# R by rows of eight tokens, W and R loaded singly, the last token's decay by one-column products, in a new order

## The chip, the cores and the metric

The kernel runs on one core of a Trainium2 chip. The time is that of one execution on the device in microseconds, the median of several runs. In a profile, PE is TensorE's matmuls, PEld its weight loads, DVE is VectorE, ACT is ScalarE, POOL is GpSimd, and SP is the engine whose queue issues most DMAs.

## What is computed

A recurrence over 768 tokens keeps a 40 x 40 state for each of 4 batches and 8 heads; its outputs go through a feed-forward block.

```python
for t in range(S):                       # S = 768, D = 40
    y[:, :, t] = np.einsum('bhd,bhde->bhe', rt, state)
    Sa = np.einsum('bhde,bhe->bhd', state, at)
    state_decay = state * wt[:, :, None, :] - np.einsum('bhd,bhe->bhde', Sa, bt)
    state = state_decay + np.einsum('bhd,bhe->bhde', vt, kt)
...
h = x @ w_in                             # x: 3072 x 320, w_in: 320 x 2048
g = np.maximum(h, 0.0) ** 2
return g @ w_out                         # 2048 x 320
```

## The kernel before

The 768 tokens are cut into 6 chunks of 128, and a chunk of one batch is a unit `m` (24 of them, in the code "batch" too). For each unit the six inputs W, K, B, A, V and R are loaded as tiles with 128 tokens on the partitions and 8 heads x 40 beside them (`NW`, `NK`, ... `NR`).

Preparation of a unit: ScalarE takes the logarithm of W (`ln`), a matmul with a triangle of ones (`cs`) sums it over the tokens into a PSUM bank, and two exponentials make the decays `GA` and `GI`. GpSimd or VectorE multiply K and B by `GI` (`kb`), and A by the decay that is shifted by one token (`aa`; from unit 6 a DMA makes the shifted `E` from `GA`). TensorE transposes A, K and B, V and R (`tA`, `tKB`, `tV`, `tR`), each by matmuls with the identity `IDb`; ScalarE or VectorE copy the results out of PSUM (`AT`, `KBT`, `VT`, `RT`). From unit 8 K and B are transposed by a DMA instead, on SP's queue. `GL` is the decay of a chunk's last token, one value for each of 320 columns with those on the partitions.

Two steps `st` per unit, of four heads each, then do the chunk's algebra: `ca` (products of 64 rows, two heads at once), the masks `CN`, the corrections `P`, `corr1`, `corr2` with `Mc`, `c1` and `Sn`, the products with R (`ex`), the masks `EVX`, the outputs and the next state (`y`, `Xn`, `us`, `UZ`). The feed-forward block of one or two units is `tx`, `XT`, `hr` (64 rows), `hp`, `hs` (relu), `Gt` (square), `op`, `osb` and the store.

TensorE has three arrangements here: the whole array (128\*128), rows cut in two (64\*128: `ca`, `ex`, `hr`), and rows and columns cut in two (64\*64: the transposes of R of units 0 to 3).

R of units 0 to 3 is loaded so that a partition holds 8 consecutive tokens of one head, a run of 320 floats; two DMAs of 64 partitions each do it (`rows`). `t_r` then makes 16 transposes of 64 by 64, and `e_r` reads the bank with a stride. R of later units is loaded with one token per partition, two units in one DMA (`two`), and `t_r` makes four transposes of 128 by 128. W's tiles are pairs of units too, two of them; a pair's tile is free for the next load when both units have used it. For units 0 to 5 `GL` comes from four matmuls of one column (`gl_mm`) that write into the bank of `cs`; from unit 6 a DMA transpose of `GA`'s last 32 tokens, one for two units, brings it into `GD`, and GpSimd or VectorE multiply that by the mask `HM`.

Each engine runs its instructions in the order that is written out in the table `ORDER`; `WAYS` says which of the possible engines makes an operation, `BANKS` which of the 8 PSUM banks it takes, and `IDLE` before which operations filler matmuls are put (`L1060`).

Of the kernel before, what the change touches and what calls it, by code (L numbers as in the profile page):

```python
# [7 lines left out]
FP32 = mybir.dt.float32  # L8
# [11 lines left out]
def kernel(  # L20
# [39 lines left out]
    RING = {"N": 3, "NW": 2, "lnW": 2, "GI": 2, "KB": 5, "GA": 2, "E": 3, "AA": 2, "V": 5, "R": 3, "SN": 8,  # L60
            "EVX": 3, "RT": 4, "VT": 4, "KBT": 3, "AT": 3, "GL": 4, "GD": 2, "CN": 3, "c1": 2, "x1": 2,
# [3 lines left out]
    SPLIT, THREE, ROWS, GLD, PAIR = 1, 6, 4, 6, 4  # L65
# [59 lines left out]
    def pe(n):  # L125
        return n, n + 0.165
# [130 lines left out]
    for m in range(NBC):  # L257
        o = Batch()
        bt.append(o)
        o.nat = bt[m - 1].nat if m % 2 else {key: buf(f"N{key}") for key in "WKBAVR"}  # L260
        o.lnW, o.hi, o.lo, o.GI, o.KB, o.AA, o.V, o.R, o.VT, o.RT, o.KBT, o.AT, o.GL, o.Xn = (
            buf(x) for x in ("lnW", "hi", "lo", "GI", "KB", "AA", "V", "R", "VT", "RT", "KBT", "AT", "GL", "Xn"))
        o.GA, o.E, o.GD = (bt[m - 1].GA, bt[m - 1].E, bt[m - 1].GD) if m % 2 else (buf(x) for x in ("GA", "E", "GD"))
# [20 lines left out]
    def add_load(m, key, rank):  # L284
        o = bt[m]
        c, bb = divmod(m, NB)

        def tile_():
            return sb(o.nat[key], [128, 2, NHH, D], FP32)

        def go():
            nc.sync.dma_start(
                out=tile_()[:, m % 2],
                in_=nat_srcs[key][bb, :, c * L:(c + 1) * L, :].rearrange("h t e -> t h e"))

        def two():
# [4 lines left out]
        def rows():  # L301
            t_ = tile_()[:, m % 2]
            src = nat_srcs[key][bb, :, c * L:(c + 1) * L, :]
            for s in range(2):
                nc.sync.dma_start(
                    out=t_[64 * s:64 * s + 64].rearrange("p i e -> p (i e)"),
                    in_=src.rearrange("(j s) (b i) e -> s b j (i e)", s=2, i=8)[s])
        if m >= PAIR and m % 2:
            alias["L", m, key] = "L", m - 1, key
            return  # L310
        op(("L", m, key), "SP", rank, 0.6, 0.6, [], [o.nat[key]],
           two if m >= PAIR else rows if key == "R" and m < ROWS else go)
        ops["L", m, key].dma = "h", 1.03

    def add_prep(m):
# [5 lines left out]
        def ln():  # L321
            t_ = sb(o.lnW, [128, NHH * D], FP32)
            nc.scalar.activation(out=t_[:], in_=o.nat["W"].tile[:, m % 2].rearrange("p h e -> p (h e)"),
# [55 lines left out]
        def gl_ev(eng, at):  # L379
            t_ = sb(o.GL, [128, PB, 2], FP32)  # L380
            engine(eng).tensor_tensor(
                out=t_[:], in1=HM[:], op=ALU.mult,
                in0=at.rearrange("p (j u) -> p j u", u=1).to_broadcast([128, PB, 2]))
        def gl_row():
            nc.sync.dma_start_transpose(out=sb(o.GD, [128, 2 * PB, 32], BF16)[:],
                                        in_=o.GA.tile[96:128].rearrange("p b h e -> p (b h e)"))
        if m < GLD:
            op(("gl", m), "PE", s0 - 0.5, *pe(0.102), [("GA", m), ("GI", m)], [o.GA, csb], gl_mm, "F")
            op(("GL", m), "DVE", s0 - 0.3, 0.075, 0.16, [("gl", m)] + cleared("HM", 0), [csb, o.GL],
               lambda: gl_ev("DVE", csb.tile[:, 320:320 + PB]))  # L390
        else:
            if m % 2:
                op(("gD", m), "SP", s0 - 2.0, 0.6, 0.6, [("GA", m - 1), ("GA", m)], [o.GA, o.GD], gl_row)
                ops["gD", m].dma = "h", 0.4
                alias["gD", m - 1] = "gD", m
            op(("GL", m), "POOL", s0 - 0.3, 0.1, 0.16, [("gD", m)] + cleared("HM", 0), [o.GD, o.GL],
               lambda eng: gl_ev(eng, o.GD.tile[:, PB * (m % 2):PB * (m % 2) + PB, 31]), alts=[("DVE", 0.075, 0.16)])
# [13 lines left out]
        def cast(key, j0, n, eng):  # L411
            h = slice(2 * j0, 2 * j0 + 2 * n)
            copy(eng, out=getattr(o, key).tile[:, h, 0:D], in_=o.nat[key].tile[:, m % 2, h])
# [102 lines left out]
        def e_r(eng):  # L516
            t_ = sb(o.RT, [128, PB, L], BF16)[:]
            if m >= ROWS:
                copy(eng, out=t_, in_=bank(b4)[:, 0:PB * L].rearrange("p (j t) -> p j t", t=L))
                return  # L520
# [3 lines left out]
           "R" if m < ROWS else "F")  # L524
# [404 lines left out]
    def add_guard():  # L929
# [32 lines left out]
        "#D!8!=!2!%!;!$!(#J!6#F!:!>!+!.#K$C!-!L!,!?!9!!!)!&#L#O!<!@!^!A#E!_!C#M!B#N#I!J!U#Q!M!7!D"  # L962
        "$I!I!E!H!5!S#G#P!O$J!T!Y!N$K%>!P!/!W!K!X#H!`#U!Z$N!a$D!r$P!3#T!b!c$O$F#X!t!V!F$Q!0!d$L#V"
        "&=!i!s!Q!e#[!f$M%A!*!R!g!u#Y!h!v#`#Z#]![!w%D!x#t!]%E#W$E#v%F#u#b$U$G!y#R!G#c%G!z#a#w#^#d"
        "!j%H%I#S!|!##e%K%B$S#f!k!}#x#_%?!~!{%P#g#y##$X$H#k$T#z!l#!($(%$R#h$Z&>!m(&#$$[$Y#{%@$V!n"
        "%J#&$a%Q$s#|&?%N#i$]#j$u&@#}%S!4#)$c#~&C%L!1%T#%(*%M$b#l$W%C$^$t$_$!$d!o&D#m!p$`$#&E!q$v"
        "&H$%$w%O$e$$#n&I$f%U#*(,$g#o$x&J$h$&$i&K#p%V&F#(((#/$y#q&M$)$j$z#r$(()#s$*%[${&G$k&L%^(+"
        "%n$l$})5%]$.$/(/#0$~&A%W$0#1%!$|%p(0(-$m%#%_&N%`%$%a(6$n%%(7(.%o&T$o&U#2%q%X$p(1%r#6$q&B"
        "%e$r#3%(%R&O(4%s#4&R(5%&#7#9%b%Y%)&S#5$+%c%t+*&n%Z);%u#=%v%d)<#:&p#+)v%f#;&o&Z):)=%*#>&]"
        "$1&P%+$2&[#8)>&q%g)w&^)7&r%h&_(2)x$3&V%j&`&s%w%x&a&Q$5&t)?(3%y&X)@&W#<(:%i&b%z&c&Y%{&#(<"  # L970
        "(;(8%|%k$6)6)y(=(9&u$4&e%}&v){%~$8%l&f#-$9&!(>&d&x)8#?(O%m&y$<(Q)z(?#,(P&g(@%,$:&h)|&((R"
        "$7&)$;(A%0$=&*(B%-(S&i+j#.(C(T+0%3(D&z)C&w*$&j&{%.%7*(%1(F(U#@&|(G+1%/+k(V&}(W(E%4&l&$&m"
        "%8(Y&k$?$>(X)~(Z)F(H%5([(J*/)B#A&~)}(!(I+2&+(^#B(#(K&&#C(]+l&/%2)I)9(g*#(_*0)J+.(h&%+3*%"
        "(`,y$@)D+5(j$-(M(c(a)G&,+4)H$A(L)O(i%6)c%9)Q(k&-*++,)e(l)M*&%:&0)d&.)E)P)N)f*))A&1*,)g++"
        ")R+m)S)h**+n)T)i(N*1)X)U*D(d*2)V)j+o%;*3)k+p)W-!*E(b)l)m&2*F%<)K*4-#+-)Y)L*5*G)n&6-]-$+q"
        "*H)Z*6)o&7+8*M&3)p+/+7)[&4*-*7*I)^*.(m+t+>(n)q(t+u*J*8(o)r*9&8(u)]+9*K(p.l*;(q)s*L(v*W,{"
        ")_*<*:)t*N)a*=*O-%&5+v+<+{-(&9+=(r)`+w*?$,*!)u+V*>+C-^)b(x+x+D-_*@(y+W&:+:+;+E(z(s,z-`*B"
        "-&+X*P*[&;({*X+r-b*A(|*R(w)!*Q/O+y-d+F-a+Y+z+?(}+A+Z*S,|+G+B+@+H+[*T*])#,~+I,#*_*^+J*`)$"
        "*U+K,7,%*a)%+L)&,$(~)*.r+]-c)(,&,8+M-++^/P+|+N+O+_,9,(-*)+*b*V,-,:*f+s))*C,;,),}+Q*c*g),"
        ",<+a-1*d,=*i+}*j+b-h,>,*+c*k,?.m,+-g+~,,*m+d(f$B,A-,+e,.,!*p+P-i*q*h-/-.+`*t*e*r-4.o-0+f"  # L980
        ",/-j+R.s-n+g-k-l.t+T-5+S--*l,B+h-6-m-I-8-2*n/Q-o-7)--p,N-J*u.q+6-9-K+U,0-:-e,C*o,1-q-;)."
        "-r,2,J-?-<.n,D-L-3-=,3,E%=->,O)//R-R,5,F,P,6,4-s(e,G.*+i)1.+,Q-M,K/S,H/T.,-N,R,@*w.p-O*s"
        ".u,S-u-P*{0d.w-t.--@..*x,I-Q-A./-S*y.0/U-B-T.})2-C*z-D.v-v*v.z.y-U,T-w*|,X-V/V-|-x.1.|,U"
# [185 lines left out]
```

## Time and profile before

| | |
|---|---|
| Median of 3 runs | 257.37 us (256.85 to 257.81) |
| Profiled execution, its own time | 256.97 us |
| Its span, first to last instruction | 255.4 us |
| Granted TensorE clock | 1.00 |
| DMA queue of SP, share of 16 engines' span | 76.5% |

A row of a group gives line, engine, operation, the tiles written and read, the number of instructions, then busy us and mean ns of one, and after the second bar the engine's idle time before them and what ended it. A row in order of time gives the start, the busy time of the merged group, engine, line and tiles. Matmuls are pipelined: the busy time of one holds its whole passage, so that what a matmul takes from TensorE is read from start to start.

### The profile page before, as it was taken

The numbers are of one execution on the slowest core, as the hardware profiler recorded it, in microseconds if no ns is written. First come the engines' busy times: TensorE is split into PE (matmuls) and PEld (weight loads), VectorE is DVE, ScalarE is ACT, GpSimd is POOL, SyncE is SP. The second block draws the span as 40 slices with busy tenths as digits, with TensorE's granted clock in tenths as the row PEclk, the third lists the DMA queues.
The fourth block names the chain that finished last, engine by engine and source line by source line (L and its number), as shares of the span: only waits on it lengthen the run. The fifth ranks groups of instructions, "written<-read, shape, count | busy, mean of one in ns | idle before, by whom it ended". The sixth has DMA issues, their size and how long they took to land.

```text
span 255.4 us, 9993 instructions
## 1 busy us (share of the span) xinstructions
PE 242.0 (95%) x3948; PEld 193.1 (76%) x3948; DVE 230.4 (90%) x556; ACT 215.6 (84%) x589; POOL 172.0 (67%) x259
## 2 busy tenths in 40 slices
PE   7978889999999999999999999999999999999993
PEld 7656667787787687887788777877788787878772
DVE  6799999998799999999999999999998898999482
ACT  3669978898698898899999999998999798877660
POOL 4366784886696969875568979995748694716340
PEclk9999999999999999999999999999999999999999
DMA  6999999999599979889988899988898989300111
GB/s 111 189 176 149 174 217 177 147 153 215 101 150 192 168 134 181 173 153 165 200 159 165 160 190 173 167 176 156 154 168 123 214 188 152 70 30 5 68 35 68
DMA packets 172256, 37.95 MB, mean 149 GB/s; under 512 B 165047, under 2 KB 170679, under 8 KB 172206
## 3 DMA queue, kind: packets, MB, share of 16 engines
q1 hardware_dynamic: 169646, 34.66, 76.5%
q0 software_dynamic: 2560, 2.62, 6.2%
q8 instruction: 31, 0.51, 0.9%
q14 instruction: 19, 0.16, 0.2%
HBM read 28.84 MB, written 3.93 MB: 128 GB/s over the span
## 4 chain that ended last, share of the span: by engine, by line
PE 51%; ACT 2%; DVE 2%; DMA 2%; issue 1%; POOL 0%; SPq 0%; POOLq 0%; DVEq 0%
PE bank L888 16%; PE bank L854 10%; PE bank L417 4%; PE bank L641 3%; PE bank L841 3%; PE bank L563 3%; PE bank L595 2%; PE bank L661 2%; DMA NA<-in_a_dram 2%; PE bank L333 1%; PE bank L669 1%; PE bank L623 1%; PE bank L816 1%; PE bank L586 1%; PE bank L628 1%
## 5 line engine op out<-in xcount | busy, mean ns | idle before, releaser
L646 DVE TENSOR_TENSOR EVX<-bank,MEX 128x512 bf16<-128x512 f32 x96 | 62.4, 683 | 1.6 <-PE bank L641 1.1
L571 DVE TENSOR_TENSOR CN<-bank,MCN 128x512 bf16<-128x512 f32 x96 | 61.3, 682 | 1.9 <-PE bank L563 1.0
L888 PE MATMUL bank<-WOUT,Gt 128*128 128x320 bf16 x384 | 59.4, 300 | 0.4 <-DMA WOUT<-in_moe_w_out_dram 0.4
L872 POOL TENSOR_TENSOR Gt<-hs 128x512 bf16<-128x512 bf16 x43 | 45.2, 1055 | 19.2 <-ACT hs L861 14.0
L854 PE MATMUL bank<-XT,WIN 128*128 128x256 bf16 (+1 forms) x448 | 54.5, 258 | 0.0
L861 ACT ACTIVATE hs<-bank 128x512 bf16<-128x512 f32 x77 | 45.5, 601 | 6.0 <-issue 2.5
L888 PEld LDWEIGHTS <-Gt 128*128 128x128 bf16 x384 | 35.4, 97 | 13.3 <-issue 0.8
L854 PEld LDWEIGHTS <-WIN 128*128 128x128 bf16 x448 | 34.8, 97 | 7.1 <-issue 3.6
L612 ACT ACTIVATE junk<-CN 128x512 bf16<-128x512 bf16 x48 | 30.6, 638 | 0.2
L341 POOL TENSOR_TENSOR lo<-hi 128x320 f16<-128x320 f32 x21 | 15.1, 720 | 15.0 <-ACT hi L237 8.5
L401 POOL TENSOR_TENSOR KB<-NB,GI 128x320 bf16<-128x320 f32 (+1 forms) x22 | 18.7, 854 | 8.3 <-ACT GI L357 6.8
L870 ACT ACTIVATE Gt<-hs 128x512 bf16<-128x512 bf16 x37 | 23.1, 636 | 1.4 <-DVE hs L863 1.4
L595 PEld LDWEIGHTS <-CN 128*128 128x128 bf16 x384 | 18.5, 96 | 5.3 <-issue 2.6
L401 POOL TENSOR_TENSOR KB<-NK,GI 128x320 bf16<-128x320 f32 x21 | 18.6, 888 | 5.5 <-ACT GI L357 5.5
L407 POOL TENSOR_TENSOR AA<-NA,E 128x320 bf16<-128x320 f32 x19 | 15.3, 809 | 10.1 <-DMA NA<-in_a_dram 7.5
L563 PE MATMUL bank<-AT,KBT 64*128 64x128 bf16 x384 | 18.0, 218 | 2.2 <-ACT KBT L237 0.7
L841 PE MATMUL bank<-XT,WIN 64*128 64x256 bf16 (+1 forms) x224 | 18.5, 256 | 0.0
L661 PE MATMUL bank<-KB,EVX 128*128 128x40 bf16 x384 | 17.2, 180 | 0.0
L563 PEld LDWEIGHTS <-KBT 64*128 64x128 bf16 x384 | 12.2, 94 | 6.6 <-issue 2.8
L750 POOL TENSOR_TENSOR x<-Mc,c 128x640 bf16<-128x640 bf16 x10 | 14.0, 1398 | 3.9 <-PE bank L641 3.8
L237 ACT ACTIVATE SNall<-bank 128x160 bf16<-128x160 f32 x38 | 11.4, 307 | 6.0 <-PE bank L595 4.5
L681 DVE TENSOR_TENSOR Xn<-bank,E 128x160 bf16<-128x160 f32 x48 | 14.7, 316 | 1.8 <-PE bank L669 0.7
(134 smaller groups left out, 652.6 us busy)
## 6 DMA issues: line engine op xcount, KB each, us to landing
out_dram<-osb SPq DMA_DIRECT2D x24, 160.0 KB, 2.4
NW<-in_w_dram SPq DMA_DIRECT2D x10, 320.0 KB, 4.5
NK<-in_k_dram SPq DMA_DIRECT2D x10, 320.0 KB, 5.5
NB<-in_b_dram SPq DMA_DIRECT2D x10, 320.0 KB, 5.1
NA<-in_a_dram SPq DMA_DIRECT2D x10, 320.0 KB, 5.2
NV<-in_v_dram SPq DMA_DIRECT2D x10, 320.0 KB, 5.3
NR<-in_r_dram SPq DMA_DIRECT2D x10, 320.0 KB, 4.9
E<-GA SPq DMA_DIRECT2D x9, 224.0 KB, 4.6
```

Of the source, the lines that this page charges most:

```text
L401: engine(eng).tensor_tensor(out=o.KB.tile[:, u, h, 0:D], in0=o.nat[key].tile[:, m % 2, h], op=ALU.mult, in1=o.GI.tile[:, h])
L563: nc.tensor.matmul(out=quads(ca[s])[:, i, u, :], lhsT=o.KBT.tile[half(s), u, j0 + i, :], rhs=o.AT.tile[half(s), j0 + i, :], start=(i == 0 ...
L571: nc.vector.tensor_tensor(out=t_[:, :, s], in0=quads(ca[s]), in1=MCN[:], op=ALU.mult)
L595: nc.tensor.matmul(out=P[:, 2 * i + s], lhsT=CN[:, i, s, 1, :], rhs=X[:, 2 * i + s], start=False, stop=last, skip_group_check=True)
L612: nc.scalar.activation(out=t_, in_=CN_.tile[:, :, :, 1, :], func=ACTF.Square, accum_out=ACC[:, AN + st:AN + st + 1])
L646: nc.vector.tensor_tensor(out=sb(EV_, [128, 2, 2, 2, L], BF16)[:, :, s], in0=quads(ex[s]), op=ALU.mult, in1=MEX[:].rearrange("p (i u) x -> ...
L841: nc.tensor.matmul(out=hv(w_)[:, u], lhsT=WIN[2][half(w_), j * 128:(j + 1) * 128], rhs=XT()[half(w_), 2, 0:nb, :], start=(u == 0), stop=False,
L854: nc.tensor.matmul(out=hv(w_)[:, u], lhsT=WIN[g][:, (j0 + u) * 128:(j0 + u + 1) * 128], rhs=XT()[:, g, 0:nb, :], start=False, stop=(g == 1 ...
L861: nc.scalar.activation(out=t_, in_=hpb.tile[:], func=ACTF.Relu)
L870: nc.scalar.activation(out=t_, in_=x_, func=ACTF.Square)
L872: engine(eng).tensor_tensor(out=t_, in0=x_, in1=x_, op=ALU.mult)
L888: nc.tensor.matmul(out=opb.tile[:, 0:DM], lhsT=Gtb[h].tile[:, j, b_, :], rhs=WOUT[:, j, :], start=(j == 0), stop=(j == NJ - 1))
```

## The change

All units load R by rows of eight tokens, so that `tR` is sixteen transposes of 64 by 64 everywhere. W and R are loaded for one unit at a time, into five tiles each. `GL` comes from matmuls of one column for all units, on VectorE, and the DMA transposes into `GD` are gone. The tables are new: the order on every engine, the choices of engines, the banks, and the fillers (66 in place of 84).

```diff
-    RING = {"N": 3, "NW": 2, ..., "GL": 4, "GD": 2, ...
-    SPLIT, THREE, ROWS, GLD, PAIR = 1, 6, 4, 6, 4
+    RING = {"N": 3, "NW": 5, "NR": 5, ..., "GL": 4, ...
+    SPLIT, THREE, PAIR = 1, 6, 4
...
-        o.nat = bt[m - 1].nat if m % 2 else {key: buf(f"N{key}") for key in "WKBAVR"}
+        o.nat = dict(bt[m - 1].nat) if m % 2 else {key: buf(f"N{key}") for key in "KBAV"}
+        o.nat.update({key: buf(f"N{key}") for key in "WR"})
...
+        two = m >= PAIR and key not in "WR"
...
         op(("L", m, key), "SP", rank, 0.6, 0.6, [], [o.nat[key]],
-           two if m >= PAIR else rows if key == "R" and m < ROWS else go)
+           rows if key == "R" else pair if two else go)
...
-        if m < GLD:
-            op(("gl", m), "PE", s0 - 0.5, *pe(0.102), [("GA", m), ("GI", m)], [o.GA, csb], gl_mm, "F")
...
-        else:
-            if m % 2:
-                op(("gD", m), "SP", s0 - 2.0, 0.6, 0.6, [("GA", m - 1), ("GA", m)], [o.GA, o.GD], gl_row)
...
+        op(("gl", m), "PE", s0 - 0.5, *pe(0.102), [("GA", m), ("GI", m)], [o.GA, csb], gl_mm, "F")
+        op(("GL", m), "DVE", s0 - 0.3, 0.075, 0.16, [("gl", m)] + cleared("HM", 0), [csb, o.GL], gl_ev)
...
         def t_r():
-            if m >= ROWS:
-                turn(bank(b4), [flat(o.R.tile[:, 2 * j:2 * j + 2, :]) for j in range(PB)])
-                return
             for i in range(8):
                 for s in range(2):
                     nc.tensor.transpose(out=b4.tile[half(s)].bitcast(BF16)[:, 64 * i:64 * i + 64],
...
-    IDLE = ((135, 29, 7), (42, 8, 1), (44, 23, 2), (90, 10, 0), (329, 6, 0), (929, 8, 5),)
+    IDLE = ((30, 14, 7), (135, 23, 7), (54, 9, 3), (163, 4, 3), (106, 6, 0), (411, 10, 2),)
```

What the tables do to the order is seen at three places. The first is TensorE at R's transposes of unit 14 (`R` is R's tile, `IDb` the identity, `CN` and `V` belong to the correction `P`, `KBT` and `AT` to `ca`). Before, they follow `P` and are followed by `tx`, all of them 128\*128:

```order
L586 LDWEIGHTS CN_353
L586 MATMUL bank_87<-V_104,CN_353 128x40
L417 LDWEIGHTS R_109
L417 MATMUL bank_86<-IDb,R_109 128x128
L417 LDWEIGHTS R_109
```

Now they stand between the two `ca` of another unit, which are 64\*128; this is where they begin:

```order
L549 LDWEIGHTS KBT_285
L549 MATMUL bank_89<-AT_283,KBT_285 128x128
L502 LDWEIGHTS R_109
L502 MATMUL bank_85<-IDb,R_109 64x64
L502 LDWEIGHTS R_109
```

Four transposes by 128 inside 128\*128 work have become sixteen by 64 inside a run of 64-row products, which goes on with the second `ca` after them.

The second place is SP's queue around the DMA transposes of units 11 and 12 (`NR` and `NW` are the tiles of R and W, `KBT` the DMA transposes that `ca` needs, `GD` the last tokens). Before:

```order
L446 DMA_TRANSPOSE KBT_618<-KB_91 128x8x128
L297 DMA NR_169<-in_r_dram 128x16x40
L385 DMA_TRANSPOSE GD_1550<-GA_96 128x8x32
L297 DMA NB_181<-in_b_dram 128x16x40
L896 DMA out_dram<-osb_1848 128x320
L297 DMA NV_235<-in_v_dram 128x16x40
L297 DMA NR_573<-in_r_dram 128x16x40
L367 DMA E_97<-GA_95 112x1024
L367 DMA E_97<-GA_95 15x1024
L446 DMA_TRANSPOSE KBT_333<-KB_92 128x8x128
```

Now:

```order
L882 DMA out_dram<-osb_1984 128x320
L296 DMA NW_385<-in_w_dram 128x8x40
L296 DMA NW_209<-in_w_dram 128x8x40
L301 DMA NB_170<-in_b_dram 128x16x40
L308 DMA NR_214<-in_r_dram 64x1x320 x2
L301 DMA NA_183<-in_a_dram 128x16x40
L370 DMA E_97<-GA_95 112x1024
L370 DMA E_97<-GA_95 15x1024
L301 DMA NA_443<-in_a_dram 128x16x40
L882 DMA out_dram<-osb_1764 128x320
L301 DMA NV_515<-in_v_dram 128x16x40
L438 DMA_TRANSPOSE KBT_285<-KB_92 128x8x128
```

One load of R for two units has become two issues for each, W comes singly, and the transposes into `GD` are gone.

The third place is VectorE where `GL` of unit 8 is made now (`Mc` and `c` belong to the corrections of a step, `hi` to the logarithm of W):

```order
L240 CAST Mc_1167<-bank_83 128x160
L242 TENSOR_SCALAR hi_185<-lnW_181 128x320
L384 TENSOR_TENSOR GL_340<-bank_84,HM 128x8
L240 CAST Mc_1167<-bank_86 128x160
L594 TENSOR_TENSOR c_1184<-bank_83,Mc_1167 128x160
```

`GL` reads the bank of the sums and stands among the evacuations; before, 14 of the 18 from unit 6 stood on GpSimd and read `GD`.

More of the change, by code (lines that the diff above doesn't have):

```diff
@@ L286, in add_load, with pair @@
         c, bb = divmod(m, NB)
+        two = m >= PAIR and key not in "WR"
         def tile_():
-            return sb(o.nat[key], [128, 2, NHH, D], FP32)
+            return sb(o.nat[key], [128, 2, NHH, D] if key not in "WR" else [128, NHH, D], FP32)
         def go():
+            t_ = tile_()
             nc.sync.dma_start(
-                out=tile_()[:, m % 2],
+                out=t_[:, m % 2] if key not in "WR" else t_[:],
                 in_=nat_srcs[key][bb, :, c * L:(c + 1) * L, :].rearrange("h t e -> t h e"))
-        def two():
+        def pair():
             nc.sync.dma_start(
@@ L305, in rows @@
                 nc.sync.dma_start(
-                    out=t_[64 * s:64 * s + 64].rearrange("p i e -> p (i e)"),
+                    out=tile_()[64 * s:64 * s + 64].rearrange("p i e -> p (i e)"),
                     in_=src.rearrange("(j s) (b i) e -> s b j (i e)", s=2, i=8)[s])
-        if m >= PAIR and m % 2:
+        if two and m % 2:
             alias["L", m, key] = "L", m - 1, key
@@ L322, in ln @@
             t_ = sb(o.lnW, [128, NHH * D], FP32)
[L323 removed]
+            nc.scalar.activation(out=t_[:], in_=o.nat["W"].tile[:].rearrange("p h e -> p (h e)"),
                                  func=ACTF.Ln)
@@ L412, in cast @@
             h = slice(2 * j0, 2 * j0 + 2 * n)
-            copy(eng, out=getattr(o, key).tile[:, h, 0:D], in_=o.nat[key].tile[:, m % 2, h])
+            x_ = o.nat[key].tile
+            copy(eng, out=getattr(o, key).tile[:, h, 0:D], in_=x_[:, h] if key == "R" else x_[:, m % 2, h])
         def turn(t_, rows):
@@ L967 @@
[L967 to L971, printed above, removed]
```

150 lines of the change are left out of this document (71 added, 79 removed).

## The prediction

> **What bounds the kernel now.** I read the page's busy shares first, then busy time by stretch (columns: stretch, its length, then busy us of PE, PEld, DVE, ACT, POOL with counts, granted clock, DMA share, GB/s), then TensorE in order of time, since a busy PE says little by itself.
>
> ```profile
> span 255.4 us, 9993 instructions
> PE 242.0 (95%) x3948; PEld 193.1 (76%) x3948; DVE 230.4 (90%) x556; ACT 215.6 (84%) x589; POOL 172.0 (67%) x259
> ...
> 0.00:10.00 10.00, 8.39 (x94) 7.50 (x95) 6.24 (x29) 3.93 (x9) 2.57 (x14) 1.00 0.79 140
> ...
> 10.00:60.00 50.00, 43.47 (x851) 34.57 (x849) 48.13 (x115) 42.76 (x123) 34.50 (x55) 1.00 1.04 173
> 60.00:100.00 40.00, 39.04 (x644) 30.74 (x642) 37.07 (x88) 34.21 (x96) 32.24 (x44) 1.00 0.96 157
> 100.00:220.00 120.00, 119.61 (x1973) 96.11 (x1971) 114.36 (x271) 113.46 (x312) 89.08 (x131) 1.00 0.93 169
> 220.00:250.00 30.00, 30.00 (x391) 23.42 (x389) 24.10 (x56) 20.83 (x51) 13.63 (x17) 1.00 0.10 33
> ...
> 60.00:252.00 192.00, 0.61 (x8) 0.49 (x8) 1.00 0.80 144
> ```
>
> The last row is that of the filler matmuls alone (`L1060`): 8 of the 84 stand after 60 us, so 76 before. Two regimes are to be seen. From 10 to 60 us TensorE is idle 50 − 43.47 = 6.5 us, while VectorE (DVE) is busy 48.13 of 50: VectorE sets the pace there, since the feed-forward matmuls that fill TensorE later don't exist yet. From 60 us TensorE is idle 0.96 us, from 100 to 250 us only 0.39. There every TensorE instruction that is added is paid in time; every one elsewhere only if it becomes late.
>
> ```profile
> 120.87 0.26 PE L595 MATMUL bank<-c,CN 128*128 128x40 bf16 x4
> 121.06 0.29 PE L641 MATMUL bank<-RT,VT 64*128 64x128 bf16 x4
> ...
> 123.64 0.62 PE L563 MATMUL bank<-AT,KBT 64*128 64x128 bf16 x16
> 124.09 0.33 PE L641 MATMUL bank<-RT,VT 64*128 64x128 bf16 x4
> ```
>
> What counts on TensorE is start to start (first column), not the busy time. The four matmuls at 120.87 and others of 40 columns start 25 ns apart, yet the next group starts 0.19 us later: 0.09 us goes to the change from a 128*128 to a 64*128 arrangement. Sixteen matmuls of 64 rows start within 0.45 us (0.028 each, in pairs).
>
> **The change, part by part.** The sum is made against the profiled execution: 256.97 us, span 255.4 and 1.6 around it. It lies 0.4 below the median of the three runs, 257.37.
>
> *R's transposes* (20 batches, from batch 4). Four 128-column transposes become sixteen of 64 by 64, as batches 0 to 3 have them already.
>
> ```profile
> 127.21 0.38 PE L417 MATMUL bank<-IDb,R 128*128 128x128 bf16 x4
> 127.43 0.33 PE L816 MATMUL bank<-IDb,Xn 128*128 128x128 bf16 x3
> ...
> 16.16 0.26 PE L586 MATMUL bank<-V,CN 128*128 128x40 bf16 x4
> 16.26 0.38 PE L417 MATMUL bank<-IDb,AA 128*128 128x128 bf16 x4
> 16.57 0.44 PE L513 MATMUL bank<-IDb,R 64*64 64x64 bf16 x16
> 16.94 0.29 PE L417 MATMUL bank<-IDb,V 128*128 128x128 bf16 x2
> ...
> 42.63 0.38 PE L841 MATMUL bank<-XT,WIN 64*128 64x128 bf16 x7
> 42.95 0.22 PE L513 MATMUL bank<-IDb,R 64*64 64x64 bf16 x2
> ```
>
> Before: 127.43 − 127.21 = 0.22 us. After: 0.37 (16.57 to 16.94), of which 0.09 is the change back to 128*128, so 0.28 for the block; 20 x 0.06 = 1.1 us, and I take 1.0. The entry costs 0.09 as well: the same four transposes of A take 0.31 to the next start at 16.26, not 0.22. Counted in the two orders, TensorE changes its arrangement 175 times before and 190 times now: excursions to 64 rows fall from 87 to 82, since R's blocks stand beside other 64-row groups, but 26 passes between 64*128 and 64*64 come in place of one. That one is the row at 42.63: seven matmuls of 64 rows, some 0.20 us at 0.028, take 0.32 to the next start, 0.12 over. So I price it like any other: 15 x 0.09 = 1.4 us. The bounds are −0.9 (26 passes cost nothing: 15 x 0.09 − 26 x 0.09) and 1.8 (0.12 each).
>
> The Trainium skill, page TensorEngine Tiling (Array Packing), section Tiling Modes, lists 64×128 and 64×64 as two configurations and says that changing the mode, not merely the tile, drains the TensorE. By that rule the 1.4 stands; were it only a change of tile, the sum would be 2.3 lower (rival 2). The single row at 42.63 is on the rule's side.
>
> *The evacuations of R's transposes* read PSUM with a stride now.
>
> ```profile
> L237 ACT ACTIVATE RT<-bank 128x512 bf16<-128x512 bf16 x21 | 12.6, 606 | 3.9 <-PE bank L513 3.1 <-PE bank L417 0.6
> L240 DVE COPY RT<-bank 128x512 bf16<-128x512 bf16 x3 | 1.5, 507 | 0.0
> ```
>
> 22 of 24 go to ScalarE, where both forms share the mean of 606 ns; the two on VectorE cost at most 0.2 each above the 416 of a plain copy. Nothing in the sum.
>
> *The last token's decay* (18 batches from 6). Four matmuls of one column replace a DMA transpose per pair of batches; VectorE makes GL.
>
> ```profile
> 14.72 0.34 PE L376 MATMUL bank<-IDb,GA 128*128 128x1 bf16 x8
> 14.92 0.30 PE L333 MATMUL bank<-hi,UTS 128*128 128x320 bf16 x1
> ...
> L381 POOL TENSOR_TENSOR GL<-GD,HM 128x8 f32<-128x8 bf16 x14 | 3.3, 234 | 0.0
> L381 DVE TENSOR_TENSOR GL<-bank,HM 128x8 f32<-128x8 f32 x6 | 0.9, 156 | 0.0
> ```
>
> Eight of them take 0.20 us, 0.025 each: 72 x 0.025 = 1.8 us on TensorE. VectorE gets 18 x 156 − 4 x 157 ns = 2.2 us, GpSimd loses 14 x 234 = 3.3.
>
> *TensorE in all:* 1.0 + 1.4 + 1.8 = 4.2 us more. Fillers fall from 84 to 66, 18 x 0.056 = 1.0; they stand where TensorE waits anyway, so I give nothing for them.
>
> *Which engine does what.* The new order also moves evacuations and products.
>
> ```profile
> L863 DVE TENSOR_SCALAR hs<-bank 128x512 bf16<-128x512 f32 x19 | 12.8, 684 | 2.8 <-ACT junk L765 2.4 <-PE bank L854 0.2
> L240 DVE COPY AT<-bank 128x512 bf16<-128x512 bf16 x15 | 6.3, 418 | 0.4 <-PE bank L417 0.4
> L692 DVE TENSOR_TENSOR UZ<-us,GL 128x160 bf16<-128x160 f32 x5 | 2.0, 405 | 0.0
> L750 DVE TENSOR_TENSOR x<-Mc,c 128x640 bf16<-128x640 bf16 x2 | 1.2, 604 | 0.0
> L861 ACT ACTIVATE hs<-bank 128x512 bf16<-128x512 f32 x77 | 45.5, 601 | 6.0 <-issue 2.5 <-DVE Gt L872 1.6 <-PE bank L595 0.8
> L237 ACT ACTIVATE AT<-bank 128x512 bf16<-128x512 bf16 x8 | 4.8, 598 | 0.5 <-PE bank L417 0.4
> L872 POOL TENSOR_TENSOR Gt<-hs 128x512 bf16<-128x512 bf16 x43 | 45.2, 1055 | 19.2 <-ACT hs L861 14.0 <-DVE hs L863 2.9 <-ACT TB L237 2.1
> L750 POOL TENSOR_TENSOR x<-Mc,c 128x640 bf16<-128x640 bf16 x10 | 14.0, 1398 | 3.9 <-PE bank L641 3.8
> ```
>
> VectorE: hs 19 to 14 (−3.4), AT 15 to 10 (−2.1), UZ 5 to 1 (−1.6), x 2 to 5 (+1.8), GL +2.2; with the twenty smaller moves, each at its group's mean, −10.6 us. ScalarE: hs +5 (3.0), AT +5 (3.0), the rest −2.0: +4.0. GpSimd: Gt 43 to 48 (+5.3), x 10 to 7 (−4.2), GL −3.3, the rest +11.4: +9.2. Up to the third feed-forward block (its first matmuls of `hr`), where TensorE has the same work behind it in both orders within 0.3 us, VectorE has 3.9 us less before it, 3.5 when the overlap of neighbouring instructions is taken off; ScalarE 0.7 and GpSimd 4.8 more. In the row of 10 to 60 us these two have 7 and 15 us free.
>
> So the opening should get shorter: 0 at least (ScalarE or GpSimd become as late as VectorE was), 3.5 at most. VectorE's 96% there is near the upper end; 2.8 is taken. From 60 to 100 us VectorE's relief can remove waits of TensorE: 0 to 2, and I take 1.0, the 0.96 idle of that row. After 100 us nothing.
>
> *Loads.* R from batch 4 comes as 40 DMAs of 80 KB with rows of 1280 bytes for 10 of 320 KB, W as 20 for 10, and 9 transposes go: 31 issues more on SP's queue.
>
> ```profile
> q1 hardware_dynamic: 169646, 34.66, 76.5%
> ...
> NW<-in_w_dram SPq DMA_DIRECT2D x4, 160.0 KB, 3.4
> NR<-in_r_dram SPq DMA_DIRECT2D x8, 80.0 KB, 3.3
> ...
> L305 SPq DMA_DIRECT2D NR<-in_r_dram x8: 579/622/5024, 2.2 to 35.9; - x8
> ...
> POOL AA L407 <- DMA NA<-in_a_dram: 7.5, 3, 3.8
> ```
>
> The packets fall by 20 x (1024 − 128) = 17,920 of 169,646, a tenth. Little waits for loads: GpSimd 7.5 us in all for A, its largest such wait, while TensorE is idle 0.39 us after 100 us. 31 issues at 0.62 are 19 us on SP. KBT's transposes and E's shifts are queued behind them, and `ca` waits for KBT; but both orders put at least 3.6 us of TensorE work between a KBT transpose and its `ca`. Zero for both, between −1 and +1.
>
> **Sum:** 256.97 + 4.2 − 2.8 − 1.0 = 257.4 us. Its own range goes from the opening at 3.5 with the loads at half their lower bound (−0.7 − 0.6) to the opening at 1.6 (+1.2), where rival 3 begins: 256.1 to 258.6.
>
> **The rivals.**
> 1. *The opening gives more.* If TensorE's idle time from 10 to 60 us falls by VectorE's 3.5, the 1.0 us of fillers goes with it, and all 2 us of later waits go too: 256.97 + 4.2 − 6.5 = 254.7. For it: VectorE at 96%. Against it: ScalarE is at 86% there already.
> 2. *The 26 passes between 64*128 and 64*64 are free.* 257.4 − 2.3 = 255.1. Against it stands the one row.
> 3. *Slower: TensorE pays, nothing comes back.* In the opening GpSimd's products (Gt at 1055 ns each) lie on the path from hs to the output matmuls, so VectorE's relief turns into waits for GpSimd, and 0.5 us of it is left. 256.97 + 4.2 − 0.5 = 260.7. It decides once the opening returns less than 1.6 us. For it: Gt's row, 14.0 us of waits for ScalarE's hs, shows that GpSimd is in that path. Against it: GpSimd is busy 69% there.
> 4. *The bank of the sums is held longer.* `cs`'s bank now stays taken until GL is made: over the 18 batches 93 us of TensorE work lie between, where 34 lay before. One wait of 0.2 us in each is 3.6: 261.0. Against it: 59 of 8 banks x 190 us is 4%.
> 5. *SP's queue is late.* 19 us more of issues, ahead of KBT: if a fifth of them shows, 257.4 + 3.9 = 261.3. Against it: the distance from KBT to `ca` above.
>
> The Trainium skill, page DMA: Bandwidth & Descriptors, section Rules for kernel authors, advises against two transfers for two partition halves, since they serialize. The rows agree so far that 80 KB takes 3.3 us to land and 160 KB 3.4; by it, rival 5 gets its chance, no more.
>
> **Chances.** Forecast 0.37, rivals 1 to 5: 0.20, 0.12, 0.22, 0.05, 0.04. A measurement here tells about 0.5% (1.3 us) from no change. Faster 0.32, within 0.37, slower 0.31. The forecast's own range is 256.1 to 258.6; to leave out no more than 2 in 10 it must reach into both signs: 254.4 to 260.8.
>
> **What would show it.** Right: R's blocks at 0.28 us plus 0.09 for each pass; the rows of one-column matmuls at 0.1 us per batch; TensorE idle from 10 to 60 us near 4; VectorE busy near 220; TensorE idle under 0.5 after 100 us. Wrong: VectorE's busy share from 10 to 60 us falls while TensorE's idle stays at 6.5 (rival 3); passes of 0.03 (rival 2); idle before `cs` or after `gl` that ends with a bank's reader (rival 4); `ca` waiting for KBT's DMA (rival 5).

## The result, and the profile after

The changed kernel takes 263.84 us, the median of 4 runs (263.02 to 264.93); before, beside it on the same chip, 257.11 (256.34 to 257.81). The ratio is 1.0265, 95% interval 1.0213 to 1.0317: slower by 6.7 us, where 257.4 was forecast and 260.8 was the end of the range. Medians in this text are of all runs of a kernel, while ratios and intervals leave out the few runs that fell in a slower state of the chip.

The page of after, its shares and its chain of work (section 4, by engine and by line):

```profile
span 261.9 us, 10655 instructions
PE 242.4 (93%) x4242; PEld 193.7 (74%) x4242; DVE 223.3 (85%) x547; ACT 220.7 (84%) x592; POOL 180.2 (69%) x265
...
PE 60%; DVE 11%; DMA 8%; ACT 5%; POOL 5%; issue 5%; SPq 3%; POOLq 0%; DVEq 0%; ACTq 0%
PE bank L874 14%; PE bank L840 13%; DMA KBT<-KB 5%; PE bank L549 4%; PE bank L627 4%; PE bank L827 3%; PE bank L409 3%; DVE CN L557 3%; PE bank L581 3%; PE bank L647 3%; DVE EVX L632 3%; PE bank L502 2%; SPq L296 2%; DMA NB<-in_b_dram 2%; PE bank L336 2%
```

TensorE is busy as long as before (242.4 against 242.0 us) in a span 6.5 us longer, so nearly all of the loss is idle time. VectorE lost 7.1 us of work, of the 10.6 forecast. In the chain the transpose into `KBT` holds 5% of the span; before's chain, which can be followed over 58% of its span only, has no row of it.

Busy time by stretch in after (columns as in the prediction):

```profile
10.00:60.00 50.00, 44.19 (x923) 36.14 (x921) 44.39 (x112) 43.80 (x128) 38.23 (x59) 1.00 1.02 182
60.00:100.00 40.00, 36.71 (x673) 29.36 (x671) 34.99 (x83) 35.39 (x95) 34.43 (x49) 1.00 0.91 169
100.00:220.00 120.00, 115.74 (x2080) 92.71 (x2076) 107.88 (x257) 108.81 (x294) 90.38 (x126) 1.00 0.85 152
```

TensorE's idle time went from 6.5 to 5.8 us in the opening, from 0.96 to 3.3 between 60 and 100, and from 0.39 to 4.3 between 100 and 220. The loss lies where a gain or nothing was expected. The list of waits tells what TensorE waits for (us in total, times, longest; a wait shows once for the weight load, PEld, and once for the matmul):

```profile
PEld L409 <- POOL AA L398: 4.2, 4, 1.8
PEld L549 <- DMA KBT<-KB: 3.5, 3, 1.4
PE bank L409 <- POOL AA L398: 3.2, 3, 1.6
PE bank L549 <- DMA KBT<-KB: 2.7, 3, 1.1
```

In the list of before, this is the only row of TensorE behind `KBT`'s DMA, and there is none behind GpSimd's `AA`:

```profile
PEld L563 <- DMA KBT<-KB: 0.3, 1, 0.3
```

In the trace of after, TensorE's large waits from 60 to 220 us are 1.43 us at 82.23 and 1.65 at 103.88 for `AA`, and 0.90 at 87.12, 1.10 at 125.45 and 0.70 at 161.45 for `KBT`: together 5.8 of the 6.2 us by which its idle time grew there. The first wait for `AA` is at 82 us; the timelines of TensorE, GpSimd and SP's queue in after show how it comes about (start, duration, engine and line; SP's duration is that of the issue, not of the transfer):

```profile
80.57 0.23 PE L661 MATMUL bank<-TB,RT 128*128 128x80 bf16 x2
82.23 0.40 PE L409 MATMUL bank<-IDb,AA 128*128 128x128 bf16 x4 [1.43 <-POOL AA L398]
```

```profile
81.39 0.79 POOL L398 TENSOR_TENSOR AA<-NA,E 128x320 bf16<-128x320 f32 x1 [1.05 <-DMA E<-GA]
```

```profile
69.82 0.59 SPq L308 DMA_DIRECT2D NR<-in_r_dram  x1
70.46 0.58 SPq L296 DMA_DIRECT2D NW<-in_w_dram  x1
71.10 0.57 SPq L301 DMA_DIRECT2D NK<-in_k_dram  x1
71.78 2.14 SPq L308 DMA_DIRECT2D NR<-in_r_dram  x2
73.96 0.59 SPq L301 DMA_DIRECT2D NV<-in_v_dram  x1
75.01 0.93 SPq L301 DMA_DIRECT2D NA<-in_a_dram  x1
76.05 3.78 SPq L370 DMA_DIRECT2D E<-GA  x2
79.88 1.16 SPq L296 DMA_DIRECT2D NW<-in_w_dram  x2
81.14 1.30 SPq L308 DMA_DIRECT2D NR<-in_r_dram  x2
82.54 1.36 SPq L438 DMA_TRANSPOSE KBT<-KB  x1
```

TensorE waits for `AA`, `AA` for `E`, and `E`'s shift got its turn on SP at 76.05. SP issues one DMA behind the other here; the shift's inputs had been ready since 73.2 us, and its second issue ended 6.6 us after that. The 1.65 us at 103.88 came about alike: `E`'s second shift was issued at 96.90 and landed at 102.05, and GpSimd, idle for 2.64 us, began `AA` at 102.21, 0.16 us after the landing as at 81.39 (the list of waits names a product of TensorE for this wait, since that ended at about the same moment). How long an issue holds SP varies: about 0.6 us is usual for a load, a `KBT` transpose of after takes 1.2 to 3.6, and one load of R took 5.3; the two shifts at 76.05 took 3.78 together. What holds an issue up was not settled. Right ahead of the `KBT` transpose at 82.54 stand the two loads of R for a later unit, whose cast starts 27 us later at the earliest.

The queue is not longer in sum. Added up over the trace, SP's 186 issues of after take 188 us, the 155 of before 196, of which the nine transposes into `GD` took 20. Once issued, the urgent transfers land as fast as before: `KBT` after 4.4 us (median; before 4.1), the two shifts of `E` after 3.9 and 3.1 (before 4.6 and 4.1). What changed is when they get their turn. Before, 15 of the 16 `KBT` transposes have landed 0.8 us or more ahead of the `ca` that reads them; in after, four land 0.11 us ahead or less, and the other twelve 1.5 us or more.

So the first reading is a theory A: SP's queue, with more issues and with loads that are not urgent ahead of urgent ones. Its rivals: B, the work on TensorE, paid in full; C, GpSimd, which took over work and delivers `AA` late; D, the new order in itself.

### The profile page after: what moved, and what is told of

Read it like the earlier page. It is cut to its first block, busy times and chain, and to the rows that moved or that the text cites. A ratio compares the mean times of both kernels' runs of the same rounds, so it can differ in the third digit from the quotient of the medians.

```text
span 261.9 us, 10655 instructions
## 1 busy us (share of the span) xinstructions
PE 242.4 (93%) x4242; PEld 193.7 (74%) x4242; DVE 223.3 (85%) x547; ACT 220.7 (84%) x592; POOL 180.2 (69%) x265
## 4 chain that ended last, share of the span: by engine, by line
PE 60%; DVE 11%; DMA 8%; ACT 5%; POOL 5%; issue 5%; SPq 3%; POOLq 0%; DVEq 0%; ACTq 0%
PE bank L874 14%; PE bank L840 13%; DMA KBT<-KB 5%; PE bank L549 4%; PE bank L627 4%; PE bank L827 3%; PE bank L409 3%; DVE CN L557 3%; PE bank L581 3%; PE bank L647 3%; DVE EVX L632 3%; PE bank L502 2%; SPq L296 2%; DMA NB<-in_b_dram 2%; PE bank L336 2%
## 5 line engine op out<-in xcount | busy, mean ns | idle before, releaser
L632 DVE TENSOR_TENSOR EVX<-bank,MEX 128x512 bf16<-128x512 f32 x96 | 63.1, 683 | 6.4 <-PE bank L627 5.7
L858 POOL TENSOR_TENSOR Gt<-hs 128x512 bf16<-128x512 bf16 x48 | 49.9, 1046 | 24.3 <-ACT hs L847 23.1
L847 ACT ACTIVATE hs<-bank 128x512 bf16<-128x512 f32 x82 | 47.7, 602 | 9.2 <-PE bank L840 5.4
L392 POOL TENSOR_TENSOR KB<-NK,GI 128x320 bf16<-128x320 f32 (+1 forms) x24 | 20.0, 834 | 5.1 <-DMA NK<-in_k_dram 5.1
L398 POOL TENSOR_TENSOR AA<-NA,E 128x320 bf16<-128x320 f32 x21 | 17.1, 821 | 9.2 <-PE bank L655 2.6
L392 POOL TENSOR_TENSOR KB<-NB,GI 128x320 bf16<-128x320 f32 (+1 forms) x23 | 19.6, 858 | 4.3 <-PE bank L581 2.7
L856 ACT ACTIVATE Gt<-hs 128x512 bf16<-128x512 bf16 x33 | 21.0, 640 | 0.7 <-DVE hs L849 0.7
L678 POOL TENSOR_TENSOR UZ<-us,GL 128x160 bf16<-128x160 f32 x31 | 14.1, 460 | 7.5 <-DVE us L672 7.5
L594 DVE TENSOR_TENSOR c<-bank,Mc 128x160 bf16<-128x160 f32 x48 | 15.0, 318 | 3.1 <-ACT TB L237 1.7
L237 ACT ACTIVATE TB<-bank 128x512 bf16<-128x512 bf16 (+1 forms) x22 | 12.9, 586 | 4.6 <-PE bank L614 2.2
```

The lines of the kernel that those rows point to most:

```text
L392: engine(eng).tensor_tensor(out=o.KB.tile[:, u, h, 0:D], in0=o.nat[key].tile[:, m % 2, h], op=ALU.mult, in1=o.GI.tile[:, h])
L632: nc.vector.tensor_tensor(out=sb(EV_, [128, 2, 2, 2, L], BF16)[:, :, s], in0=quads(ex[s]), op=ALU.mult, in1=MEX[:].rearrange("p (i u) x -> ...
L847: nc.scalar.activation(out=t_, in_=hpb.tile[:], func=ACTF.Relu)
L858: engine(eng).tensor_tensor(out=t_, in0=x_, in1=x_, op=ALU.mult)
```

## The experiments

Medians of 4 runs (e7 10, e17 and e18 12); before, on the same chips, had medians of 256.88 to 257.85.

### R's edit taken apart, in after's order and in before's

e1, plain loads of R, 64x64 transposes kept:

```diff
-           rows if key == "R" else pair if two else go)
+           rows if key == "R" and m < 4 else pair if two else go)
```

> After, but R of units 4 to 23 is loaded plainly by one DMA each (a token per partition) instead of two with rows of 8 tokens; the transposes stay 64x64, so R of these units reaches the product in another arrangement (its tokens are mixed up; nothing else is changed). SP has 20 issues less (about 12 us of its queue). Theory A (SP's queue, made longer by 31 issues, brings KBT, E and K late; their waits on TensorE in the trace of after are some 3 to 6 us): 258 to 261. Theory B (the work on TensorE costs its full 4 us, and the waits belong to the new order's engines): 263.8, no change. Theory D (the new order itself): 263.8.

e2, loads by rows kept, transposes as before; e3 is e1 and e2 together:

```diff
         def t_r():
+            if m >= 4:
+                turn(bank(b4), [flat(o.R.tile[:, 2 * j:2 * j + 2, :]) for j in range(PB)])
+                return
...
```

> After, with R still loaded by rows in two DMAs, but turned by four full 128x128 transposes and copied plainly for units 4 to 23 (R of these units reaches the product in another arrangement). TensorE loses 20 x 0.05 of block time and 15 changes of arrangement at 0.09: 2.4 us. Theory A: 261.5 or more, since the waits behind DMAs stay. Theory B: 261.4, the 2.4 come back whole. Theory D: between 261.4 and 263.8, part of it lost in waits.

> After with both undone for units 4 to 23: R loaded plainly by one DMA and turned by four 128x128 transposes; computes the reference. W singly, the decay by products and the new order stay. Theory A: 256 to 259. Theory B: 261.4. Theory D: 262 to 264: the R edit is not where the loss is.

e4, before with R by rows and 64x64 transposes for all units:

```diff
-           two if m >= PAIR else rows if key == "R" and m < ROWS else go)
+           rows if key == "R" else two if m >= PAIR else go)
...
```

`rows` now makes the four DMAs of both units of a pair.

> Before, in before's order, with R by rows for all units: the load of a pair becomes four DMAs, the transposes 64x64 (computes the reference). SP has 30 issues more, TensorE 20 x 0.05 and some 20 to 30 changes of arrangement at 0.09 more. Theory A: 261 to 264, the same loss as after. Theory B: 259.5 to 261 (2.4 to 3.5 us over before). Theory D: 257 to 259, most of after's loss is not in R.

e5 and e6 are its two halves: the transposes alone, the loads alone.

> Before, in its order, with the 64x64 transposes for R of all units but R still loaded by pairs (R of units 4 to 23 reaches the product with its tokens mixed up; nothing else is changed). Only TensorE's work grows: in the trace of the run with R by rows on before it was 3.0 us more in changes of arrangement and 1.0 in the blocks. Theory B (TensorE's work is paid in full and is the whole cost of R): 264 to 265, as with the rows. Theory A (the longer SP queue has the other half): 261 to 261.5. Theory C (a unit's late products take the added work as cover): below 260.

> Before, in its order, with R loaded by rows of 8 tokens (four DMAs for a pair in place of one, 30 issues more) but turned by 128x128 transposes as before (R of units 4 to 23 reaches the product with its tokens mixed up). Only SP's queue and the transfers change. Theory B: 257.4, no change. Theory A: 260.5 to 262, half or more of the 7.7 us of R by rows on before.

| run | us | against after (263.84) or before | ratio to before, interval |
|---|---|---|---|
| e1 after, plain loads | 261.96 | −1.9 | 1.0144 [1.0065, 1.0223] |
| e2 after, 128x128 | 262.23 | −1.6 | 1.0121 [1.0021, 1.0220] |
| e3 after, R undone | 260.81 | −3.0 | 1.0112 [1.0028, 1.0197] |
| e4 before, R's edit | 265.06 | +7.7 | 1.0315 [1.0231, 1.0398] |
| e5 before, 64x64 alone | 260.87 | +3.4 | 1.0118 [1.0054, 1.0183] |
| e6 before, loads alone | 262.19 | +4.8 | 1.0206 [1.0130, 1.0282] |

R's edit alone costs before 7.7 us, as much as the whole change, and it has two halves that nearly add (3.4 + 4.8 = 8.2). For the transposes alone (e5) TensorE's added work, expected at 4.0, accounts for the cost. For the other half TensorE's work is the same, and the loads alone cost 4.8 us although they make the DMA engines' work smaller: in e6 the hardware queue's packets fall from 169,646 to 152,206, and the share of 16 engines' time from 76.5% to 71.7%. In after's order the halves are worth 1.9 and 1.6: the loads less than theory A expected, the transposes near theory B's 2.4. The intervals of both touch after's (1.0213 to 1.0317), so neither is clear by itself; the 3.0 of e3 is. With R undone 3.4 us over before were left.

### W, and the new order alone

e7, before with W of a pair in two DMAs:

> Before, in its order, with W of a pair loaded by two DMAs one behind the other in place of one (10 issues more on SP, 6 us of its queue); computes the reference. Theory A (every issue on SP counts, some 0.1 us each in the runs so far): 258 to 259.5. Theory B and theory D: 257.4, no change.

258.50 us, ratio 1.0038 [0.9997, 1.0079]: 1.1 us over before by the medians, not told from nothing, and 2.0 at the upper end.

e8, after's order with all edits undone as far as possible:

```diff
-            for j in range(PB):
+            for j in range(1):
...
```

These are the one-column products. W comes by one DMA for both units of a pair, into three pair tiles, and R as in e3.

> After's order with the other edits undone as far as its list of steps allows: R loaded plainly and turned by 128x128 transposes, W loaded by pairs, and one of four one-column products for the decay (the decay of the first pair of heads is used for all four; of 294 added instructions on TensorE 24 stay). Theory D (the order itself makes the products late): 259 to 260.5, close to the 260.8 with R undone. Theory B: 257 to 258.5, as before, since 1.8 us of one-column products go. Theory A: 257 to 259, since the 10 issues for W go as well.

265.64 us, ratio 1.0333 [1.0247, 1.0420], outside all three expectations and 4.8 over e3. It does not isolate the order: after's order issues some of W's loads only 3 us ahead of their logarithms, and a load twice as large probably comes too late there. The list of waits of e8:

```profile
ACT lnW L327 <- DMA NW<-in_w_dram: 8.9, 5, 4.1
```

In after the same line has 2.9 us. It suggests that this order lives on W's single loads, no more.

### Issues without bytes, and all the work in before's order

e9, thirty tiny DMAs on before:

```diff
+            if key == "R":
...
+                for x in range(3):
+                    i = 3 * (m // 2 - 2) + x
+                    nc.sync.dma_start(out=few[0][:, i:i + 1], in_=r[bb, 0, 0:16, 0:1])
```

> Before, with three more DMAs behind each pair's load of R (30 in all), each of 16 single numbers into a small tile that nothing reads; computes the reference. SP has as many issues as with R by rows, at the same places, and hardly a byte more moves. Theory A1 (the issues themselves hold up what stands behind them in SP's order): 261 to 262.5, as the 262.2 of the rows turned by 128x128. Theory A2 (the transfers by rows, half a tile each, are what is late): 257 to 258.5.

265.72 us, ratio 1.0268 [1.0167, 1.0370]: some 7 us over before (6.9 by the ratio, 4.3 to 9.5 by its interval) for 30 issues that move 64 bytes each. That is beyond A1's range. Issues that move next to no bytes cost as much as the loads by rows did in e6, so A2, by which only the transfers are late, does not hold; whether the transfers by rows add anything of their own is not shown. The waits in e9 are of the same kinds as those of after:

```profile
PEld L571 <- DMA KBT<-KB: 2.7, 5, 1.4
PEld L425 <- POOL AA L415: 1.9, 1, 1.9
PE bank L425 <- POOL AA L415: 1.6, 1, 1.6
PE bank L571 <- DMA KBT<-KB: 1.4, 3, 1.0
```

And its queue, around 98 us:

```profile
95.29 0.55 SPq L299 DMA_DIRECT2D NA<-in_a_dram  x1
95.89 2.17 SPq L299 DMA_DIRECT2D NR<-in_r_dram  x1
98.10 2.19 SPq L307 DMA_DIRECT2D few<-in_r_dram  x3
100.34 0.59 SPq L375 DMA_DIRECT2D E<-GA  x1
100.97 0.58 SPq L299 DMA_DIRECT2D NV<-in_v_dram  x1
101.73 2.13 SPq L454 DMA_TRANSPOSE KBT<-KB  x1
```

Three tiny issues take 2.19 us of SP (1.27 the first, 0.42 each of the others), and `E`'s second shift and a `KBT` transpose stand right behind. They land at 103.39 and 105.86; in before's trace the same two land at 100.49 and 102.98.

e10, before's order with the work of all three edits (e4, e7, and four one-column products beside each of R's transposes):

> Before's order with the work of all three edits in it: R by rows and turned 64x64 (7.6 us alone), W of a pair in two DMAs (1.1 alone), and four one-column products per unit from unit 6 on beside R's transposes (72 x 0.025 = 1.8; their result is not used, the decay still comes by its transposing DMA); computes the reference. If the costs add and the new order is not the cause (theories A and B): 267 to 269, so that the new order of after (263.8) would have given some 4 us back. Theory D (the new order is what loses): 263 or less.

265.87 us, ratio 1.0302 [1.0240, 1.0365]. The sum of the parts did not come: e4's 265.06 hardly rises when 72 products and 10 issues are added. After does nearly this work (without the nine transposes into `GD`) in 2.0 us less, not 4, and the two intervals overlap.

### GpSimd, and the one-column products

e11, `AA` of units 6 to 23 on VectorE:

```diff
+            if o.name[0] == "aa" and o.name[1] >= 6:
+                o.eng = "DVE"
```

> After, with the products AA = A x E of units 6 to 23 all on VectorE, none on GpSimd (14 to 17 of them move: GpSimd loses some 0.8 us each, VectorE gains some 0.4 each); computes the reference. Theory C (GpSimd, which took over work from VectorE, delivers AA late: TensorE's waits for AA are 3.7 us in the trace of after): 260 to 262. Theory A (AA waits for E, whose DMA is late): 263 to 264.5, no gain.

268.04 us, ratio 1.0354 [1.0247, 1.0461]: theory C gets no support. The gain that it expected did not come, though VectorE's added 0.4 us per unit may hide one. The trace of after speaks more plainly: GpSimd stood idle for 1.05 and 2.64 us before the two `AA` that TensorE waited for longest, and began each 0.16 us after `E`'s shift had landed.

e12, R undone and one product in place of four:

> After with R undone (plain load, 128x128 transposes), and one of the four one-column products for the decay (the decay of the first pair of heads is used for all four). 72 instructions on TensorE go, as many as the edit added. Theory B (0.025 us each, paid in full): 259.0, 1.8 below the 260.8 with R undone. If they fill waits: 260.8. What then is left over before's 257.4 (1.6 or 3.4) belongs to W and to the order.

262.86 us, ratio 1.0174 [1.0096, 1.0253], where e3 had 1.0112 [1.0028, 1.0197]. The 1.8 us did not come back; the intervals overlap, and a loss by leaving work out is not claimed. The products cost TensorE 0.10 us a unit, as the timeline of after shows (TensorE's instructions start at 114.49 and 114.59); that they fill time in which it would wait anyway fits, but is not shown.

```profile
114.49 0.24 PE L379 MATMUL bank<-IDb,GA 128*128 128x1 bf16 x4
114.59 0.33 PE L802 MATMUL bank<-IDb,Xn 128*128 128x128 bf16 x3
```

### Issues taken off SP

e13 and e14, the 24 stores issued by GpSimd; e15 and e16, one shift of 127 rows in place of two:

```diff
-                nc.sync.dma_start(out=out[tok:tok + L, :], in_=osbb.tile[:])
+                nc.gpsimd.dma_start(out=out[tok:tok + L, :], in_=osbb.tile[:])
```

> After with the 24 stores of the result issued by GpSimd in place of SP, at the same places of the order; computes the reference. SP loses 24 issues (some 14 us of its queue), GpSimd gains 24 issues of 0.57 to 0.8 us. Theory A (SP's queue): 259 to 262, 2 to 5 us back. Theory D (the new order): 263 to 265, GpSimd's issues cost a little.

> Before with the 24 stores issued by GpSimd in place of SP; computes the reference. Theory A: 253 to 256, as thirty issues more cost 8 us. If before's order has slack on SP that only more issues use up: 257 to 259.

> After with each shift of GA to E by one DMA of 127 rows in place of two of 112 and 15; computes the reference. SP has 9 issues less, none on another engine. Theory A: 260.5 to 262.5 (at 0.15 to 0.3 us an issue). Theory D: 263.8. If the DMA of 127 rows takes longer than the one of 112, AA comes later: 264 to 266.

> Before with each shift of GA to E by one DMA of 127 rows; computes the reference. Theory A: 255 to 256.5. Otherwise 257 to 258, or 258 to 260 if the one DMA takes longer.

270.35 (1.0544 [1.0447, 1.0640]), 271.42 (1.0569 [1.0503, 1.0634]), 336.65 (1.3075 [1.2986, 1.3164]) and 338.91 us (1.3194 [1.3110, 1.3278]). All four missed every expectation and say nothing on the theories, since each put a cost of its own in place of SP's. In e15 one line holds most of the 73 us over after:

```profile
POOL AA L401 <- DMA E<-GA: 67.1, 8, 10.2
```

TensorE is idle 76 us there, against 19.5 in after, and busy 18 us longer at a granted clock of 0.89. The transfer of 127 rows is what the rest waits for; the two of 112 and 15 rows are no whim.

e17 and e18 therefore take issues off SP and put nothing in their place:

```diff
-           rows if key == "R" and m < 4 else ...
+           tile_ if key == "R" and m > 5 else rows if key == "R" and m < 4 else ...
...
```

> After with R undone (128x128 transposes) and R of units 6 to 23 not loaded: the tile keeps an earlier unit's R, everything behind it runs as before. SP loses 18 issues and the DMA engines 18 transfers against the run with R undone (260.8). Theory A (SP and its transfers hold the rest): 256.5 to 258.5. Theory D (the order): 260 to 261.

> Before, with R of units 6 to 23 not loaded (the tile keeps an earlier pair's R): 9 issues and 9 transfers of a pair less. Theory A, if before too is held by SP: 254.5 to 256.5. If before has slack there that only more issues use up: 257 to 257.5.

e17: 255.16 us, ratio 0.9897 [0.9865, 0.9929]; 5.7 us under e3, beyond A's range. e18: 257.40 us, ratio 0.9971 [0.9943, 1.0000]. With 18 loads of R gone, after's order is faster than before; before itself gains nothing. So the 3.4 us that R's undoing left hang on R's loads in SP's queue too, and D falls as far as it means the order of the computing engines: without these loads, after's order is the faster one. The order of SP's queue, however, is part of the new tables. e3 has 11 issues more than before, and its issues take less of SP's time (187 against 196 us); whether the 3.4 us come of the number of issues or of the places where the loads stand, no run separates. e17's stretches and TensorE's waits for `KBT`, with no row left for `AA` on GpSimd:

```profile
10.00:60.00 50.00, 45.72 (x905) 37.12 (x903) 45.46 (x117) 44.55 (x131) 38.95 (x62) 0.97 1.06 184
60.00:100.00 40.00, 38.57 (x689) 31.69 (x689) 38.19 (x92) 38.02 (x102) 38.00 (x53) 1.00 0.94 156
100.00:220.00 120.00, 118.22 (x1971) 94.35 (x1968) 111.03 (x262) 112.33 (x304) 93.16 (x128) 1.00 0.77 135
```

```profile
PEld L555 <- DMA KBT<-KB: 0.4, 1, 0.4
...
PE bank L555 <- DMA KBT<-KB: 0.3, 1, 0.3
```

TensorE's idle time is 4.3, 1.4 and 1.8 us in the three stretches (after: 5.8, 3.3, 4.3). Its queue around the same transpose of unit 8:

```profile
65.04 1.56 SPq L301 DMA_DIRECT2D NV<-in_v_dram  x1
66.64 1.92 SPq L301 DMA_DIRECT2D NA<-in_a_dram  x1
71.29 1.43 SPq L370 DMA_DIRECT2D E<-GA  x2
72.77 1.17 SPq L296 DMA_DIRECT2D NW<-in_w_dram  x2
74.79 1.37 SPq L438 DMA_TRANSPOSE KBT<-KB  x1
```

Here SP stands idle from 68.56 to 71.29, the two shifts take 1.43 us instead of 3.78, and the transpose's issue ends 1.4 us after its inputs are ready, where it was 6.0 in after. e17 takes away issues and transfers alike; how much of its 5.7 us each has in after's order was not tried. No kernel of this study that does the whole work is faster than before.

## Why the prediction was wrong, point by point

- **The loads, priced at zero between −1 and +1: this is the step that failed.** It rested on the distance between a `KBT` transpose and its `ca` in the program's order, at least 3.6 us of TensorE work. But the order says where an issue stands, not when SP comes to it: the one at 82.54 was issued 4.6 us after its inputs were ready. And 3.6 us would not cover a transpose issued in time, since it lands 4.1 us after its issue in before and 4.4 in after (medians). In place of zero, TensorE's waits behind `KBT` and `AA` took 5.8 us from 60 to 220 us. Loads of R with a lead of 20 us and more looked harmless because they are early; for the queue an early load ahead of an urgent one is a delay. The 19 us of added issues, 31 at 0.62, did not come either: SP's issues take 188 us in all, where before's took 196.
- **Rival 5 had the right mechanism, with a chance of 0.04 and a fifth of 19 us, 3.9.** It missed by sum and place: not more time on SP, but urgent transfers that are issued later. On before, 30 issues without bytes cost some 7 us, 0.23 each; R's loads by rows 4.8.
- **The opening, −2.8.** Of TensorE's 6.5 us of idle time 0.7 went. Two waits of after, 0.77 us at 41.59 and 1.25 at 45.63, are behind casts of R and V that waited for their loads. In e17, without R's later loads, the idle time falls to 4.3, "near 4" as forecast: the relief was there, and late loads took it back. VectorE's busy time came down to 223 us, where "near 220" was forecast.
- **The waits from 60 to 100 us, −1.0, and "after 100 us nothing".** They grew by 2.3 and by 3.9, the 5.8 us above among them.
- **TensorE's 4.2.** The unit prices hold (20 x 0.06 is 1.2, not 1.1, which changes nothing). In the timeline of after R's block and its passes read:

```profile
171.07 0.44 PE L502 MATMUL bank<-IDb,R 64*64 64x64 bf16 x16
171.44 0.62 PE L549 MATMUL bank<-AT,KBT 64*128 64x128 bf16 x16
...
184.94 0.29 PE L627 MATMUL bank<-RT,TB 64*128 64x128 bf16 x4
185.16 0.44 PE L502 MATMUL bank<-IDb,R 64*64 64x64 bf16 x16
185.53 0.29 PE L627 MATMUL bank<-RT,VT 64*128 64x128 bf16 x4
```

  Block and pass from 64\*64 to 64\*128 take 0.37 us, 0.28 + 0.09, and the pass in (185.16 − 184.94 = 0.22, of which four matmuls take 0.11) costs 0.11: rival 2 falls, and the Trainium skill's rule that a change of mode drains the TensorE (TensorEngine Tiling (Array Packing), section Tiling Modes) agrees with these rows. From start to start, R's transposes take 8.9 us in after where they took 6.3, and the one-column products 2.7 where they took 1.0: 4.3 together, close to the forecast 4.2. But the fillers, for which nothing was given, take 1.7 less, and the other groups 2.2 less, so that TensorE's busy time grew by 0.4 only. This term was too high by almost 4 and hid a part of what the waits cost. Of the parts, R's 2.4 showed as 1.6 (e2), and the products' 1.8 did not show (e12).
- **Rival 3, GpSimd in VectorE's place at 260.7:** its sign came (from 10 to 60 us VectorE's busy time fell from 48.1 to 44.4, and TensorE's idle time stayed at 5.8), but it is not what made the kernel slower: the opening's idle time did not grow, and TensorE's waits for `AA` after 60 us begin with `E`'s DMA. That it, too, came out on the slow side is luck. **Rival 4**, the bank of the sums, was not tried by itself; after 60 us, TensorE's only wait over 0.15 us before `cs` is one of 0.17 at 167.41.
- **The Trainium skill's advice against two transfers for two halves of the partitions** (DMA: Bandwidth & Descriptors, section Rules for kernel authors) went the way of the measurement: e6, where four DMAs of 64 partitions took the place of one of 128, lost 4.8 us on before. That the two transfers serialize, the reason given there, no run here shows to be the cause; e9 had the same loss from issues alone.

## What to carry to other kernels

Follow every urgent transfer on an in-order DMA queue: when its inputs are ready, when it is issued, when it lands, when it is read. Then ask of each new issue what stands behind it: a load may be as early as it likes and still be harmful when a transpose or a shift that an engine waits for is queued behind it. The sum of issue times does not tell; here it fell while the kernel got slower. A kernel can have just enough room on such a queue, so that taking issues away brings nothing (e18) and adding thirty tiny ones costs 2.7% (e9). And before a price is taken as paid in full because an engine is never idle, ask whether the change gives that engine new waits: here the waits were nearly the whole cost.

## What the runs showed of the hardware

- An issue on SP takes 0.42 us for 16 numbers (median of the 30 in e9) and 0.58 for a load of 160 or 320 KB as a rule, a transpose of K and B 1.2 at the least; single issues of after hold SP for up to 5.3 us. When an issue of after starts, 2.9 of SP's transfers are on their way on average, and an issue takes 1.3 us in the mean with two on their way, 0.9 with three and 1.0 with four, so the number on the way does not explain the long ones.
- A copy within SBUF of 127 rows in one DMA is slow: in e15 its reader starts 13.1 us or more after the issue, where 112 and 15 rows land in 3.9 and 3.1 us (the medians of after). Why was not tried.
- Stores issued by GpSimd cost it 0.57 us each. In e14 VectorE's busy time grows by 7.5 us for the same instructions. The 1277 ns of `UZ` in the row below, 405 in before, is a mean that one instruction makes: it took 4.55 us and began 0.06 us after a store's issue had ended, while the other four took 0.32 to 0.67. That the stores are the cause is likely but rests on this order in time alone.

```profile
L692 DVE TENSOR_TENSOR UZ<-us,GL 128x160 bf16<-128x160 f32 x5 | 6.4, 1277 | 0.0
```
